# Tap products over a zeroed tile, a memset on another engine, and a new hand order in a one-core mixer kernel

## The chip, the cores and the metric

The kernel runs on one core of a Trainium2 chip. A core has five instruction queues that run side by side and meet only through semaphores: TensorE (PE, matrix products into PSUM; its weight loads are listed apart as PEld), VectorE (DVE), ScalarE (ACT), GpSimd (POOL) and SyncE (SP, which here only starts DMA transfers). Each queue works strictly in the order in which its instructions were written. The metric is the device time of one execution in microseconds; the reference point is the median over several executions.

## The reference

Two branches read the same tensor `q` (2048 tokens of 640 channels) and are mixed by a gate per token:

```python
x = A_q
g = sigmoid((x * gate_w).sum(-1, keepdims=True))
# branch a
k_shift = sum over t of k_pad[:, t:t+S, :] * shift_k[:, ks-1-t]      # ks = 4 taps
kv = k_shift * v
y = irfft(rfft(kv, 2S) * rfft(ssm_k, 2S))[:, :S] + kv * ssm_D         # a long convolution
a = q * y
# branch b
h = gelu(layernorm(x) @ w1)             # 640 -> 640, then four channel groups shifted by +1, -1, +2, -2 tokens
x1 = x + shifted(h) @ w2                # 640 -> 640
b = x1 + gelu(layernorm(x1) @ w3) @ w4  # 640 -> 1536 -> 640
out = g * a + (1 - g) * b
```

Inputs and output are bf16.

## The kernel before

`build` writes the work down as 784 tasks (one to twenty-odd instructions each), numbered as they are added. Each task has a name, an engine or a choice of engines, what it reads, writes and needs in buffers, and a duration for the planner. `ORDER` (lines 36 to 66) is one long hand-kept list of these numbers, with a letter behind a number where the task takes another than its first engine (`a` ACT, `v` DVE, `p` POOL). All tasks are emitted in that order, so `ORDER` fixes the order within every engine's queue. `Plan.place` (lines 147 to 220) goes through the list once with the planned durations and hands out the buffers: PSUM has eight banks, used singly or in pairs (pool `U`).

The same pass decides how many **fill** products are put ahead of a task on PE. A fill (lines 254 to 256) multiplies a tile of zeros, `FZ`, by itself, 128 rows by 512 columns, into a PSUM bank that nobody reads; it only keeps PE occupied while it would wait. Their number is the planned waiting time divided by a planned fill time: 0.43 us up to the planned moment `WARM` = 7.5 us, 0.22 us after it. Fills end when task `w1.0.0` has taken over the bank.

The stages, by task name:

- **Start.** `ldx` loads `q` by pairs of token tiles, `ldsk` loads the long filter `ssm_k` in five blocks, `ldw1`, `ldw2...`, `ldk`, `ldv` the rest; a number of small tasks on POOL, DVE and ACT make the identity, the all-ones tile `ONE`, and the table of cosines `TRIG` (`phase`, `phsmall`, `phand`, then `sin` on ACT).
- **Taps.** `ldCJ` loads `shift_k` as one row of 2560 values in one partition (tile `CJR`). For each tap j, `cjb.j` (line 484) multiplies the first row of `ONE` by that row on PE, which copies the tap to all 128 partitions of PSUM (512 and 128 columns, array rows 1 of 128); `cj.j` evacuates it to SBUF.
- **Layer norm 1.** `st1` (statistics, ACT or DVE), `rs1` (POOL), `nm1` (normalise, ACT or DVE), `tr1` (ten PE transposes), `ev1`/`evh` (evacuation of the transposed tile and of its shifted copy).
- **Filter.** `trh.cb` is 32 PE transposes of a block of `ssm_k`, `evt` evacuates; `s1h` and `s1hr` are the first transform step of the filter, `e1h` its evacuation.
- **Branch b.** `w1.G.part` and its gelu `g1`, then `w2`, `x1` (DVE, adds the product to `x`), `sq`, `ve2`, `st2` (POOL), `nm2`, `dt2` (DMA transposes), `w3`, gelu `g2`, `w4`, `t2`.
- **Branch a.** `kv3` to `kv0` on DVE: eight passes each over 128 x 2560 values, which form `k_shift * v`; `kz` zeroes the three leading rows of `K` in one partition, which only `kv0` reads (its taps j > 0). Then `s1x`, a round trip through DRAM (`wFx`, `rF`), `s2`, the products `pa`/`pb`, `s3`, another round trip (`wG`, `rG`), `s4`, and the last DVE steps `yq`, `ad`, `ax`, `fo` and the stores `st`.
- `bperm` permutes the cosine table (128 x 2048) for a DMA transpose `dbt` that `s4` needs; in the kernel before it runs on POOL (`701p`), and `kz` too (`4p`).

In the order before, PE's queue starts `fill cjb.0 cjb.2 cjb.3 cjb.1 trh.3 sgm trh.0 tr1.0 tr1.2 trh.4 trh.1 tr1.14 trh.2 tr1.4 w1.0.0`, and SP's queue `ldCJ ldx0 ldx4 ldx14 ldx2 ldsk3 ldsk0 ldgw ldx6 ... ldw1`. `sgm` (line 679) is a small product of the gate's weights, which `ldgw` loads.

Of the kernel before, what the change touches and what calls it, by code (L numbers as in the profile page):

```python
# [10 lines left out]
ACT = mybir.ActivationFunctionType  # L11
ALU = mybir.AluOpType
BF16 = mybir.dt.bfloat16
# [23 lines left out]
0 5 14 12 26 28 25 2 8 9 3 1 7 10 75p 68v 13 21 65p 27 6 42 86v 84v 39 69 22a 17 76v 24 18a 15 16a 58v 56v 19  # L37
66a 71v 11 400 212 29 67 38 77 78a 79 23 43 401v 81v 87 70a 57 80a 36 394 20a 40 59 395v 72 74v 41 94v 37 82 92a
61v 83v 402 85 73a 60a 88v 403a 396 397v 62 63v 93 398 89a 64a 96a 95 399v 33 97v 32 213 90 124 44 91a 47 457
128 118v 458a 119 125 116v 408 46 30 461 463 98 99v 130 129 117 404 100v 101 464a 462a 102v 35 34 407 104v 31  # L40
131 126 132 121v 405 103 445 127 465 133 453 466a 105v 146 120v 140 45 54 454a 446a 141 143 106 147 137 107v 459
144 138 110a 108a 409 410 145 111 113v 49 411 154 460a 155 152 148 149 150 109 134 153 451 449 151 468 165 112a
135 412 452a 159 450a 467 166 122 406 139 114 136 156 123a 413 115v 160 51 447 142 218 157 469 48 219 414 214
215 475 470a 222v 448a 50 473 53 168 170 476a 456 471 417 418 419 169 474a 220a 477 176 472a 172 177 162 478a
174 163 224 173 455 420 416 481 487 171 221 225 175 421 226v 488a 483 216 484a 480 187 188 181 182 482a 479 164
223 415 184 185 485 489 228a 190 422 423 424 493 4p 427 486a 490a 227 501 428 429 430 192 52 229 194 191 198
494a 497 502a 193 495 199 196 230 491 498a 492 197 195 499 200 201 496a 431 203 204 500a 432 426 505 425 158 161
506a 231 250 251 248 262 433 434 504 511 509 503 249 236 438 244 510a 512a 245 437 439 440 441 442 237 238 239
55 513 246 443 514a 247 517 436 435 444 507 508a 252 253 519 234 520a 235 523 524a 240 515 241 242 525 518a 516
521 232 206 207 526a 522a 243 178 527 263 209 528 210 233 264a 529 167 533 534v 530a 731 535 268 536a 531 532v  # L50
537 538a 265 205 208 260 540 256 269 539 258 211 179 254 266v 267 270v 272v 271 356 701p 183 261 273 186 546 541
562 217 189 312 313 202 180 306 316v 307 314v 547 308a 257 549 259 573 255 350 274 550v 542 548a 544 545v 280
310a 275 276 543a 563 281 565 574 282 277 557 309 564a 575a 292 551 578 552 594 558 560 283 566v 293 559v 561a
605 278 279 351 352v 576 579 581 582a 580v 577a 296 567 317 284 553 311 297 285 555a 568 554v 288 595 583 606
608 289 584 607a 315 609a 610 294 295 357 318 596v 589 626 611 613 614v 340 612a 637 585 360v 586v 319 713 590
642 341 615 587a 286 591a 569 592 287 330 571v 616 570a 593a 290 621 331 597 598a 638 643 338 556 599 644a 639v
353 600 320 339 321 640 645 641a 646v 291 334 622 627 572 628a 623v 629 336 601 630v 624 602v 335 354a 603a 653
674 647 332 617 625a 337 619a 658 648 358a 669 355 685 588 618a 298 631 632 299 654 655v 604 702 333 656 328
657a 659 661 322 660a 662v 670 329 620 675 676a 672 323 324 671v 690 633 325 673v 634a 635v 326 663 677 649 664
361 327 346 679 636 359 678a 686 650a 651a 665 652 687a 666a 680 688 347 667v 691 681 668 692a 689v 695 693 694a  # L60
683a 342 696 697 682a 684 699a 698v 343 300 700 304 344 302 345 305 301 303 730 712 735 703 732 736 733 362 717
# [22 lines left out]
class Plan:  # L84
# [62 lines left out]
    def place(self, order):  # L147
# [8 lines left out]
        for i in order:  # L156
# [33 lines left out]
            else:  # L190
                d = t.dur
                if e == "PE":
# [162 lines left out]
def build(env, nc, io):  # L355
# [19 lines left out]
    def dma(name, nbytes, fn, issue=0.58, **kw):  # L375
        return add(name, "SP", issue, fn, nbytes=nbytes, **kw)
# [41 lines left out]
    add("kz", {"POOL": 1.7, "DVE": 0.6}, 0, lambda t: (nc.vector if t.on == "DVE" else nc.gpsimd).memset(env["K"][0:1, 0:3, :], 0.0),  # L418
# [620 lines left out]
```

## Time and profile before

| what | us |
|---|---|
| executions of the kernel before | 231.32, 231.49, 232.72 |
| median | 231.49 |
| the profiled execution, its own time | 232.78 |
| its span, from the first instruction to the last | 231.0 |
| PE idle behind its first transposes, up to its last product | 3.5 |
| DVE idle in 0 to 20, 20 to 40, 40 to 60, 60 to 80, 80 to 100 | 4.9, 3.5, 1.9, 0.6, 0.3 |
| ACT idle in the same stretches | 7.2, 2.2, 1.8, 3.3, 1.0 |

How to read the profile: its page gives busy times, the span in 40 slices, the chain of work that ended last, and groups of instructions by source line. An answer of the trace by line L256 is the fills (recorded at the helper's line), L487 the tap products, L796 the filter's transposes, L562 the transposes of `x`, L637 and L641 `w1`, L663 `w2`, L851 and L864 the first transform step, L757 `w3`, L771 and L778 `w4`. Times in a chain and in a timeline are microseconds from the start of the span. Busy matmul times overlap, so the distance between starts, which the chain shows, is the price of a matmul in a stream. A figure in brackets at the end of a timeline row is the idle time ahead of that instruction and what ended it.

### The profile page before, as it was taken

What the parts mean: (1) busy time and instruction counts of PE and PEld (TensorE: products, weight loads), DVE (VectorE), ACT (ScalarE), POOL (GpSimd) and SP (SyncE); (2) the same over time, 40 slices, a digit from 0 to 9 for tenths busy, and PEclk for the clock granted to TensorE, in tenths of its full rate; (3) what the DMA queues carried; (4) which work ended last, traced back from release to release, by engine and by line L of the source; (5) the groups of instructions that cost most, each with busy time, mean ns of one, the idle gap of its engine ahead of it and who ended that gap; (6) DMA issues with size and microseconds to landing.
All of it is one profiled execution on the core that took longest, in us unless ns stands there. A gap on an engine that the chain in (4) does not pass through costs nothing.

```text
span 231.0 us, 5209 instructions
## 1 busy us (share of the span) xinstructions
PE 222.0 (96%) x2077; PEld 105.0 (45%) x2077; DVE 190.9 (83%) x269; ACT 154.0 (67%) x223; POOL 44.6 (19%) x92
## 2 busy tenths in 40 slices
PE   7999989999997999999999999999999999999992
PEld 1268834545443343344543333334344554445551
DVE  7949598899999999999468999898986238788993
ACT  4894799988988799979558898897965000532000
POOL 5378055513071007006421000000000000000000
PEclk9999999999999999999999999999999999999999
DMA  4999997099897899977999997999964496789623
GB/s 141 273 349 328 280 265 249 3 292 207 279 286 157 280 267 351 324 258 210 196 334 322 222 362 168 237 409 290 281 208 152 140 371 225 219 264 305 173 64 85
DMA packets 41450, 56.74 MB, mean 246 GB/s; under 512 B 15953, under 2 KB 31570, under 8 KB 41426
## 3 DMA queue, kind: packets, MB, share of 16 engines
q1 hardware_dynamic: 41426, 56.41, 84.3%
q8 instruction: 16, 0.26, 0.5%
q14 instruction: 8, 0.07, 0.1%
HBM read 34.90 MB, written 18.35 MB: 231 GB/s over the span
## 4 chain that ended last, share of the span: by engine, by line
PE 89%; DVE 5%; ACT 2%; POOL 1%; issue 1%; DVEq 0%; POOLq 0%; ACTq 0%
PE PS L757 24%; PE PS L771 17%; PE PS L663 10%; PE PS L637 7%; PE PS L898 5%; PE PS L256 5%; PE PS L796 4%; PE PS L926 4%; PE PS L851 3%; PE PS L778 3%; PE PS L641 2%; PE PS L964 2%; PE PS L562 1%; DVE QO L984 1%; PE PS L487 1%; DVE W L978 1%
## 5 line engine op out<-in xcount | busy, mean ns | idle before, releaser
L764 ACT ACTIVATE h2T<-PS 128x512 bf16<-128x512 f32 x48 | 27.8, 602 | 25.5 <-PE PS L757 22.4
L771 PE MATMUL PS<-W,h2T 128*128 128x512 bf16 (+1 forms) x288 | 40.1, 299 | 0.0
L387 ACT CAST FS<-PS 128x1024 bf16<-128x1024 f32 x38 | 37.3, 1016 | 3.3 <-issue 1.4
L757 PEld LDWEIGHTS <-W 128*128 128x128 bf16 x240 | 21.0, 98 | 31.0 <-issue 9.6
L771 PEld LDWEIGHTS <-h2T 128*128 128x128 bf16 x288 | 22.2, 98 | 18.8 <-issue 1.5
L387 ACT CAST XH<-PS 128x1024 bf16<-128x1024 f32 x24 | 23.9, 1014 | 8.2 <-PE PS L898 7.4
L757 PE MATMUL PS<-x1nT,W 128*128 128x512 bf16 x120 | 29.2, 380 | 0.0
L757 PE MATMUL PS<-XB,W 128*128 128x512 bf16 x120 | 28.3, 380 | 0.0
L913 DVE TENSOR_TENSOR PP<-XH 128x2048 bf16<-128x2048 bf16 x20 | 23.5, 1218 | 0.3
L816 DVE TENSOR_TENSOR VC<-K,VC 128x2560 bf16<-128x2560 bf16 x16 | 23.5, 1485 | 0.2
L663 PE MATMUL PS<-W,hsT 128*128 128x512 bf16 (+1 forms) x160 | 23.2, 299 | 0.0
L389 DVE CAST XH<-PS 128x1024 bf16<-128x1024 f32 x16 | 19.4, 1221 | 3.0 <-PE PS L898 2.5
L637 PE MATMUL PS<-xnT,W 128*128 128x512 bf16 x80 | 19.1, 380 | 1.1 <-ACT hsT L654 0.7
L786 DVE TENSOR_TENSOR x<-PS,x 128x640 bf16<-128x640 f32 x12 | 9.6, 821 | 11.6 <-PE PS L771 11.5
L730 POOL TENSOR_TENSOR r<-v,MH 128x2 f32<-128x2 f32 x8 | 8.2, 1021 | 54.8 <-DVE v L725 52.1
L820 DVE TENSOR_TENSOR VC<-VC 128x2560 bf16<-128x2560 bf16 x12 | 17.9, 1490 | 0.2
L663 PEld LDWEIGHTS <-hsT 128*128 128x128 bf16 x160 | 12.7, 98 | 11.5 <-issue 1.1
L970 DVE SCALAR_TENSOR_TENSOR W<-PS,GG,QO 128x640 bf16<-128x640 f32 x16 | 13.4, 877 | 2.0 <-PE PS L964 2.0
L387 ACT CAST GS<-PS 128x1024 bf16<-128x1024 f32 x13 | 13.0, 1017 | 2.9 <-PE PS L926 2.7
L256 PE MATMUL PS<-C 128*128 128x512 bf16 x32 | 13.0, 548 | 1.2 <-DVE C L477 1.2
L654 ACT ACTIVATE hsT<-PS 128x512 bf16<-128x512 f32 x20 | 11.6, 609 | 3.8 <-PE PS L637 2.4
L778 PE MATMUL PS<-W,h2T 128*128 128x128 bf16 (+1 forms) x96 | 13.6, 299 | 0.0
(110 smaller groups left out, 300.5 us busy)
## 6 DMA issues: line engine op xcount, KB each, us to landing
FH<-FS SPq DMA_DIRECT2D x8, 640.0 KB, 4.4
FXD<-FS SPq DMA_DIRECT2D x8, 640.0 KB, 5.5
FX<-FXD SPq DMA_DIRECT2D x10, 512.0 KB, 6.2
FX<-FH SPq DMA_DIRECT2D x10, 512.0 KB, 6.1
GX<-GD SPq DMA_DIRECT2D x8, 640.0 KB, 5.0
W<-in_B_w_dram SPq DMA_DIRECT2D x2, 1920.0 KB, 10.6
GD<-GS SPq DMA_DIRECT2D x8, 480.0 KB, 5.5
x<-in_A_q_dram SPq DMA_DIRECT2D x16, 160.0 KB, 4.0
```

The costliest lines, as they stand in the source:

```text
L256: nc.tensor.matmul(env.PS[:, t.fill_at, :], lhsT=Z[:, 0:128], rhs=Z[:], start=True, stop=True)
L387: nc.scalar.copy(out=out, in_=in_)
L389: (nc.vector if t.on == "DVE" else nc.gpsimd).tensor_copy(out=out, in_=in_)
L637: nc.tensor.matmul(m[:, b, :], lhsT=W[:, 0, kb, 160 * fb:160 * fb + 128], rhs=rhs(kb, shifts[fb]), start=(kb == 0), stop=(kb == 4))
L663: nc.tensor.matmul(m[:, c0:c1], lhsT=env["hsT"][:, o.buf["hs"][0], fb, 128 * (s % 4):128 * (s % 4) + 128], rhs=env["W12"][:, 1, fb, c0:c1] ...
L757: nc.tensor.matmul(env.PS[:, t.buf["U"][0], :], lhsT=env["W3"][:, kb, 128 * fb:128 * fb + 128], rhs=env.nT(int(nP[-1]))[:, :, kb, :], star ...
L764: nc.scalar.activation(out=env["h2T"][:, o.buf["h2"][0], fb, :], in_=env.PS[:, t.buf["U"][0], :], func=ACT.Gelu_apprx_tanh)
L771: nc.tensor.matmul(m[:, c0:c1], lhsT=env["h2T"][:, o.buf["h2"][0], fb, 128 * (s % 4):128 * (s % 4) + 128], rhs=env["W4"][:, fb, c0:c1], st ...
L778: nc.tensor.matmul(env.PS[:, t.buf["U"][0], 0:c1 - c0], lhsT=env["h2T"][:, o.buf["h2"][0], fb, 128 * (s % 4):128 * (s % 4) + 128], rhs=env ...
L816: nc.vector.tensor_tensor(out=VC[:, o], in0=env["K"][:, a + 3 - j:a + 7 - j, :], in1=w, op=ALU.mult)
L820: nc.vector.tensor_tensor(out=VC[:, 1], in0=VC[:, 1], in1=VC[:, 2], op=ALU.add)
L913: nc.vector.tensor_tensor(out=env["PP"][:, o.buf["PP"][0], a, :].rearrange("p (b c) -> p b c", b=2), in0=X.unsqueeze(1).broadcast_to([P, 2 ...
```

## The change

1. **Tap products.** The tile `CJR` now has 128 partitions. A new task `cjz` on ACT copies the zero tile `FZ` five times over it (128 x 2560); `ldCJ` then loads the taps into its first partition, and each `cjb.j` multiplies all of `ONE` (128 x 128 ones) by all of `CJR`, so that 127 rows of zeros are added. Its mode in the planner is that of the full products. `ldCJ` has to wait for `cjz`, which has to wait for the memset of `FZ`.
2. **Fills.** The rule that put at least two fills ahead of every `cjb` is gone, and while the planned time is below `WARM` the number of fills is taken at 0.85 of the planned wait.
3. **Memset.** `kz` may run on DVE only, and stands second in DVE's queue.
4. `bperm` may no longer run on POOL; the order puts it on DVE.
5. **Order.** All of `ORDER` is new, with other engines for some of the tasks.

```diff
-                            t.fill = int((at - max(free[e], 0.8)) / FILL_US[0])
+                            t.fill = int(0.85 * (at - max(free[e], 0.8)) / FILL_US[0])
...
-                    if self.kept is not None and t.name[:3] == "cjb":
-                        t.fill = max(t.fill, 2)
...
-    add("kz", {"POOL": 1.7, "DVE": 0.6}, 0, lambda t: (nc.vector if t.on == "DVE" else nc.gpsimd).memset(env["K"][0:1, 0:3, :], 0.0),
+    add("kz", "DVE", 0.55, lambda t: nc.vector.memset(env["K"][0:1, 0:3, :], 0.0),
...
-    dma("ldCJ", 5120, lambda t: nc.sync.dma_start(out=env.early("CJR", [1, 4 * D], BF16), in_=io["sk"].rearrange("d j -> (d j)").unsqueeze(0)),
+    add("cjz", "ACT", 2.2, lambda t: nc.scalar.copy(out=env.early("CJR", [P, 4 * D], BF16).rearrange("p (a b) -> p a b", b=512),
+                                                    in_=env.early("FZ", [P, 512], BF16).unsqueeze(1).broadcast_to([P, 5, 512])),
+        use=[zeros], w=["CJR"], roles=("C0",))
+    dma("ldCJ", 5120, lambda t: nc.sync.dma_start(out=env.early("CJR", [P, 4 * D], BF16)[0:1, :], in_=io["sk"].rearrange("d j -> (d j)").unsqueeze(0)),
         w=["CJR"], roles=("C0",))
...
-                nc.tensor.matmul(env.Uf(t.buf["U"][0])[:, c0:c1], lhsT=env["ONE"][0:1, :], rhs=row[:, j, c0:c1], start=True, stop=True)
-        tb = add(f"cjb.{j}", "PE", 0.3, cjb, r=["CJR", "c0"], use=[fill], acq=("U",), mode="r32", roles=("C0",))
+                nc.tensor.matmul(env.Uf(t.buf["U"][0])[:, c0:c1], lhsT=env["ONE"][:], rhs=row[:, j, c0:c1], start=True, stop=True)
+        tb = add(f"cjb.{j}", "PE", 0.3, cjb, r=["CJR", "c0"], use=[fill], acq=("U",), mode="f", roles=("C0",))
...
-    add("bperm", {"ACT": 2.5, "DVE": 1.4, "POOL": 3.5}, 0, lambda t: copy(
+    add("bperm", {"ACT": 2.5, "DVE": 1.4}, 0, lambda t: copy(
```

What the new order does to each queue, read from the two lists (numbers behind the new task are one higher, 785 in all):

- **PE** starts `fill sgm cjb.3 cjb.1 cjb.0 trh.4 cjb.2 tr1.2 trh.0 trh.1 tr1.0 trh.2 trh.3 tr1.14 tr1.4 s1h.4 w1.0.0`. Ahead of `w1.1.0` now stand also `w2.0`, `w2.2`, `w2.3`, `tr1.8` and `s1h.5`, and no longer `s1hr.0`. `w2.15` stands behind `s1x.0`, `s1x.3` and `s1xr.0`. The places where one kind of product (rows and columns of the array in use) follows another are 117 instead of 121.
- **SP** starts `ldx2 ldx0 ldx14 ldgw ldCJ ldsk4 ldx4 ldw2b2 ldsk0 ldsk1 ldw2b3 ldx6 ldw2b0 ldD ldsk2 ldsk3 ldw1`; `ldw1` is its 17th task as before.
- **ACT** starts `cjz warm st1.3 st1.0 cj.1 cj.3 sin cj.2 cj.0 evt.4 nm1.0 st1.7 ev1.0 evt.2 st1.6 e1h.4 ev1.14 e1h.5 g1.0.0`. Up to `g1.1.0` it has `cjz`, three `st1`, one `evt` and one `ev1` more than before, and four `nm1` and one `evh` fewer.
- **DVE** starts `zeros kz warm0 phase1 phase0 phsmall phand`. In all it has five `nm1`, four `nm2`, one `evh`, `kz` and `bperm` more, and one `st1`, two `ev1`, one `evt` and one `e3` fewer. `bperm` stands behind `e1x.1`, ahead of `ve2.6` and `nm2.5`.
- **POOL** loses `kz` and `bperm`.

More of the change, by code (lines that the diff above doesn't have):

```diff
@@ L42 @@
[L42 to L46, printed above, removed]
@@ L484, in cjb @@
         def cjb(t, j=j):
-            row = env.early("CJR", [1, 4 * D], BF16).rearrange("o (d j) -> o j d", j=4)
+            row = env.early("CJR", [P, 4 * D], BF16).rearrange("o (d j) -> o j d", j=4)
             for (c0, c1) in ((0, 512), (512, 640)):
-                nc.tensor.matmul(env.Uf(t.buf["U"][0])[:, c0:c1], lhsT=env["ONE"][0:1, :], rhs=row[:, j, c0:c1], start=True, stop=True)
-        tb = add(f"cjb.{j}", "PE", 0.3, cjb, r=["CJR", "c0"], use=[fill], acq=("U",), mode="r32", roles=("C0",))
+                nc.tensor.matmul(env.Uf(t.buf["U"][0])[:, c0:c1], lhsT=env["ONE"][:], rhs=row[:, j, c0:c1], start=True, stop=True)
+        tb = add(f"cjb.{j}", "PE", 0.3, cjb, r=["CJR", "c0"], use=[fill], acq=("U",), mode="f", roles=("C0",))
         add(f"cj.{j}", {"ACT": 0.7, "DVE": 0.82}, 0, lambda t, tb=tb, j=j: copy(t, env["VC"][:, 3, j, :], env.Uf(tb.buf["U"][0])[:, 0:D]),
```

45 lines of the change are left out of this document (25 added, 20 removed), and 8 rows, old and new, of the table ORDER.

## The prediction

> **What bounds the kernel now.** I read the page first, then the chain of waits.
>
> ```profile
> PE 222.0 (96%) x2077; PEld 105.0 (45%) x2077; DVE 190.9 (83%) x269; ACT 154.0 (67%) x223; POOL 44.6 (19%) x92
> PEclk9999999999999999999999999999999999999999
> ```
> ```profile
> 8.09 0.65 PE PS L487 x2
> 8.74 5.80 PE PS L256 x15
> 14.54 1.92 PE PS L796 x32
> ...
> 19.59 0.22 PE PS L256
> ```
> ```profile
> L256 PE MATMUL PS<-C x32: 379/619/634, 1.2 to 24.7; 128*128 128x512 bf16 x32
> ```
>
> PE is busy for 96% of the span, but not with work that counts: nothing except fills and taps runs on it before 14.54. So two things can make this kernel shorter: an earlier first transpose, or fewer holes behind it. The 15 fills ahead of 14.54 take 5.80 us, 0.39 each; one at 19.59 takes 0.22, and recorded durations of the same instruction go from 379 to 634 ns. PE thus ran at about half speed until shortly before 14.54, although the PEclk row says full speed throughout; that row does not show this brake. The planner costs fills behind 7.5 us at 0.22, so these 15 ran far longer than it planned. Was there data to work on?
>
> ```profile
> 1.12 5.03 SPq L382 DMA_DIRECT2D x<-in_A_q_dram  x8
> 6.20 1.06 SPq L510 DMA_DIRECT2D SK<-in_A_ssm_k_dram  x2
> 7.30 0.43 SPq L493 DMA_DIRECT2D GW<-in_gate_w_dram  x1
> ```
> ```profile
> SK<-in_A_ssm_k_dram SPq DMA_DIRECT2D x1, 512.0 KB, 3.9
> ```
>
> The last row is the DMA view cut to the filter block issued at 6.20: it landed 3.9 us later, at 10.1. The first transpose could have begun there and began 4.4 us later, behind queued fills. Next, how full the others are:
>
> ```profile
> 0.00:20.00 20.00, 18.73 (x118) 8.34 (x119) 15.11 (x40) 12.78 (x21) 12.04 (x42) 1.00 0.84 266
> 20.00:40.00 20.00, 19.29 (x220) 12.17 (x218) 16.50 (x35) 17.79 (x22) 9.21 (x19) 1.00 0.96 278
> 60.00:80.00 20.00, 18.75 (x148) 8.23 (x141) 19.36 (x22) 16.75 (x25) 4.67 (x4) 1.00 0.92 252
> 100.00:120.00 20.00, 18.95 (x153) 9.88 (x151) 15.06 (x32) 13.14 (x26) 6.22 (x11) 1.00 0.94 251
> ```
>
> The columns are stretch, length, then busy PE, PEld, DVE, ACT, POOL. DVE has 8.4 us free in the first 40 us and 0.6 in 60 to 80; ACT has 9.4 free in the first 40. PE's holes behind 14.54 sum to 3.5 us: 0.7 in 20 to 40, 1.25 in 60 to 80, 1.05 in 100 to 120 and 0.5 later. A gain at the start reaches the end only if DVE, nearly full from 60 us on, also starts its long passes earlier; its free time lies where it waits for PE, so it can.
>
> **The change, part by part, against the profiled 232.78.** *The start.* SP's first issue is at 0.72; eight `x` issues took 5.03, so the new order's six take 3.8; `ldgw` adds 0.43, the taps' load some 0.35, and `ldsk4` goes out near 5.4. With 3.9 to landing the first block is there at 9.3. `trh.4` also stands behind `sgm` and three taps, and three pairs of taps fill the PSUM that the fill bank leaves, so one must be evacuated first.
>
> ```profile
> x<-in_A_q_dram SPq DMA_DIRECT2D x3, 160.0 KB, 3.2
> ```
> ```profile
> GW<-in_gate_w_dram SPq DMA_DIRECT2D x1, 1.2 KB, 5.6
> ```
> ```profile
> L387 ACT COPY HT<-PS 128x2048 bf16<-128x2048 bf16 x1 | 1.9, 1866 | 0.0
> L387 ACT COPY xnT<-PS 128x1280 bf16<-128x1280 bf16 x3 | 3.7, 1225 | 3.6 <-DVE xnT L389 3.5
> L387 ACT CAST VC<-PS 128x640 bf16<-128x640 f32 x4 | 2.7, 686 | 3.6 <-PE PS L487 3.6
> L425 ACT ACT_TABLE_LOAD x1 | 1.3, 1283 | 0.7 <-PEq L1023 0.7
> L477 DVE MEMSET C<- 128x256 uint32 x1 | 0.3, 272 | 0.0
> ```
>
> The gate's weights, issued near 4.5, land between 7.7 (3.2 to landing, as the `x` loads issued early) and 10.1 (5.6, as `ldgw` itself among later traffic); the three taps take 3 x 0.65, the first evacuation overlaps all but 0.69 at most. So `trh.4` starts between 10.3 and 12.8. Two things more can hold it: half speed, which makes its 1.92 us nearly twice that, and fills, whose number the new planner pass sets and which I have not worked out. The best case is 10.3, a gain of 4.2; the worst is 14.5, none. I take 11.5 and full speed soon after it: **3.0 gained**, nearer to the landing rows than to the old start.
>
> The new wait is `ldCJ` behind `cjz`. Both longer ACT copies differ by 0.64 us over 768 columns, so 2560 columns cost 1866 + 512 x 0.83 = 2.3 us. It starts when `FZ` is cleared, near 1.15, or behind a table load at 2.0, and ends at 3.5 to 4.3; SP comes to `ldCJ` near 4.9. So it waits for nothing; were it late, `ldsk4` and all later loads in SP's queue would be late by as much. `kz` on DVE: 960 words against 256 in 272 ns make 1.0 us. It delays DVE's chain of phases by that much, with one `st1` (1.15 us) given to ACT in return; what covers it is DVE's free time in the first 20 us. Without that cover it costs 1.0 once.
>
> *The stage behind it.* Up to `g1.1.0` ACT has more to do. With 2.3 for `cjz`, 1.87 and 1.23 for `evt` and `ev1`:
>
> ```profile
> L541 ACT ACTIVATE JK<-x 128x640 bf16<-128x640 bf16 x5 | 3.7, 738 | 0.0
> L542 ACT ACTIVATE JK<-x,SA 128x640 bf16<-128x640 bf16 x5 | 4.1, 828 | 0.2
> L554 ACT ACTIVATE xn<-x,NB,RS 128x640 bf16<-128x640 bf16 x6 | 5.4, 916 | 0.0
> 39.49 0.63 ACT L654 ACTIVATE hsT<-PS 128x512 bf16<-128x512 f32 x1
> ```
>
> Three `st1` are 3 x 1.57, nearly 2 each with their read-outs, so 5.9; four `nm1` fewer save 3.7, the halo copies 1.4. The balance is 2.3 + 1.9 + 1.2 + 5.9 - 3.7 - 1.4 = 6.2, against 9.4 free. It fits, with 3.2 to spare. DVE's sum up to `kv0.v` is equal within 0.5 us (five `nm1`, one `evh` and `kz` more; two `ev1`, `evt` and `st1` fewer). `ldw1` is SP's 17th task as before: no gain or loss. I put nothing down for this stage, and its risk into a rival.
>
> *`kz` and `bperm` off POOL.*
>
> ```profile
> 68.24 1.69 POOL L418 MEMSET K<- 1x1920 bf16 x1
> 68.33 1.78 DVE L556 TENSOR_SCALAR xn<-x,r,SB 128x640 bf16<-128x640 bf16 x1 [0.40 <-POOL SB L732]
> 70.03 0.80 DVE L670 SCALAR_TENSOR_TENSOR x<-PS,x 128x640 bf16<-128x640 f32 x1
> 70.90 0.40 PE L864 MATMUL PS<-HT,TRIG 64*128 64x128 bf16 x8 [0.91 <-DVE x L670]
> ```
> ```profile
> L556 DVE TENSOR_SCALAR xn<-x,r,SB x9: 428/442/2156, 59.2 to 138.0; 128x640 bf16<-128x640 bf16 x9
> ```
> ```profile
> 41.42 1.36 PE PS L663 x10
> ...
> 105.36 13.16 PE PS L771 x96
> ```
>
> A normalisation that otherwise takes 0.44 took 1.78 while POOL cleared `K`'s rows, and ended 0.18 after POOL did. The `x` sums behind it came 1.34 late, and PE stood 0.91 us waiting for them and 0.34 more behind that, the 1.25 of this stretch. With the memset elsewhere that hole should close, unless in the new order another wait ends last there: between 0 and 1.25, I take **1.0**, since it is a direct link. The slowest of the nine, 2.16, ran beside `bperm` on POOL and lost 1.72 to it. On DVE a copy of that size from PSUM takes 1.23:
>
> ```profile
> L389 DVE COPY HT<-PS 128x2048 bf16<-128x2048 bf16 x4 | 4.9, 1225 | 5.9 <-PE PS L796 5.9
> ```
>
> So `bperm` costs DVE 1.2 and gives back 1.7, and it stands where PE has 13.16 us of `w4` ahead of it: nothing. Without that cover, 1.2.
>
> *The hole at 103 to 105.* `w2.15`, 1.36 us like every `w2`, now stands between the first `s1x` and the last two, where PE waited 1.05: between 0 and 1.05, **0.5**.
>
> ```profile
> 36.96 1.19 PE PS L637 x5
> ...
> 63.65 1.08 PE PS L637 x5
> ```
>
> *Changes of kind.* Five products behind another kind take 1.19, behind their own 1.08: 0.11 each. Four fewer: 0.4, of which **0.3** lie behind the start.
>
> *New holes.* The order is new everywhere, so waits that were covered can open. Their bounds are none and the 3.5 us of the old order; I take **1.2 lost**. The sum is 3.0 + 1.0 + 0.5 + 0.3 - 1.2 = 3.6, from 232.78 to 229.2. The profiled execution lies 1.29 above the median of 231.49. I count half of that for the clock's start, which this change also touches, and so take 0.6 off: **228.6**.
>
> **The rivals.** *The clock stays late.* If PE idles ahead of `sgm` or a tap, or the fills are still too many, the first transposes run slow or begin near 14.5. For it speaks that 15 unbroken fills took 5 us to bring full speed, and that nothing forces fills now; against it, that all-row products replace one-row ones. Then only the later terms count (1.0 + 0.5 + 0.3 - 1.2 = 0.6), with the 0.6 to the median: 232.78 - 0.6 - 0.6 = 231.6.
>
> *ACT takes over the first 40 us* (the slower side). The place is ACT's queue up to `g1.1.0`; the price is 6.2 us more work plus 1.28 if the zero copy brings a table load of its own. It decides when ACT's free time before that gelu cannot fall below 3.2: queue order counts, since `st1.7` and `st1.6` wait for the sixth load ahead of `ev1.0` and the gelus. If none of the 9.4 is used, `g1.1.0` moves from 39.5 to 47.0, while the PE work newly put ahead of it (three `w2` of 1.36, and smaller steps) excuses 4.1: 3.4 late, and the hole at 70 is then no gain: 232.78 + 3.4 - 0.6 = 235.6. With 3.4 of it used, nothing is lost or won.
>
> *Transposes do not count.*
>
> ```profile
> L562 PE MATMUL PS<-ID,xn x80: 219/219/230, 18.9 to 53.3; 128*128 128x128 bf16 x80
> ```
>
> If the transposes start slow and do not bring full speed themselves, the five `trh` (5 x 1.92 = 9.6 us fast) take twice that, 9.6 more against the 3.0 won: 232.78 + 6.6 - 0.6 - 0.6 = 238.2. Against it, the 13 us from 14.54 on are nearly all transposes, and none of the 80 of `x`, which begin at 18.9, took over 230 ns. The Trainium skill, TensorE: Matmul & The Clock Gate, Part 4, says that transposes do not count as busy for the gate and that full speed does not engage in them. By that rule this rival would come true whenever the taps end before the clock is up; the trace bears it out badly, since by the rule the speed should have fallen in those 13 us.
>
> *Everything fits:* 4.2 + 1.25 + 1.05 + 0.4 without new holes, 6.9 less: 225.3.
>
> **How the numbers follow.** Forecast 0.55, clock late 0.20, ACT 0.13, transposes 0.04, everything fits 0.08. The forecast's own spread is 226.5 to 230.5. About 1% (2.3 us) is what a measurement can tell from no change, so faster means below 229.2: two thirds of the forecast, all of the last case and a tenth of the late clock, together 0.47; slower (above 233.8) is transposes and most of ACT, 0.15; the rest, 0.38, is the same. The range of 226.0 to 232.6 leaves out the transposes, most of ACT and half of the best case, under 0.2.
>
> **What would show it.** Right: the first L796 row at 10 to 12.5; `L637` beginning near 25; no DVE row of L556 above 0.5 us; no hole at `x L670` before `w1.3`; the first gelu before 30. Wrong: fills in a long row up to 14, L796 pieces of 3 us or more, ACT's first `L654` at 32 or later, or PE holes of more than 3.5 us behind the start.

## The result and the profile after

The kernel after takes 228.88 us (median of six executions, 228.79 to 230.59), the kernel before, in the same comparison, 231.9 (231.32 to 232.86, six executions). The ratio is 0.9883, with a 95% interval of 0.9843 to 0.9922: 3.0 us faster, against a forecast of 228.6. The profiled execution of after took 228.79 with a span of 227.0, that of before 232.78 with 231.0; its traces thus differ by 4.0, a little more than the medians. Four later executions lie far off the others of their kernels and enter no ratio (545.41 of the kernel before, 427.45 of `b_cap4`, 256.63 of `b_taps`, and 424.77 of `a_first`, which was its profiled one, so that its trace isn't read); they move the medians below by some 0.1 us.

Lines of after are one higher than before's from the tap products on (L488 taps, L638 `w1`, L797 the filter's transposes), and the fills stand at L254. First the page, then PE's timeline of the start (start, duration, engine, line, operation, tiles, count, and in brackets the idle time ahead and what ended it):

```profile
PE 216.4 (95%) x2051; PEld 105.9 (47%) x2070; DVE 188.7 (83%) x275; ACT 155.4 (68%) x222; POOL 35.2 (15%) x90
```
```profile
1.17 4.92 PE L254 MATMUL PS<-C 128*128 128x512 bf16 x12 [1.17 <-DVE C L475]
8.02 0.17 PE L683 MATMUL PS<-GW,ONE 128*128 128x5 bf16 x1 [1.93 <-DMA GW<-in_gate_w_dram]
8.04 1.86 PE L488 MATMUL PS<-C,ONE 128*128 128x512 bf16 x6
...
10.69 1.99 PE L797 MATMUL PS<-ID,SK 128*64 128x128 bf16 x32
...
13.39 1.02 PE L254 MATMUL PS<-C 128*128 128x512 bf16 x4
...
27.09 1.24 PE L638 MATMUL PS<-xnT,W 128*128 128x512 bf16 x5
```

The same view of before, its first transposes and its first `w1` product:

```profile
14.47 1.99 PE L796 MATMUL PS<-ID,SK 128*64 128x128 bf16 x32
...
28.02 1.24 PE L637 MATMUL PS<-xnT,W 128*128 128x512 bf16 x5
```

The first transposes come 3.8 us earlier, but the first product with `w1` only 0.9 earlier: most of the early start is gone 16 us later. Between the two, PE before had its transposes lined up and took 13.6 us; PE after takes 16.4. By the starts in the timeline some 1.0 of these 2.8 us are work that the new order put in between (`cjb.2` 0.7 and `s1h.4` 0.3), 0.8 are waits and 0.6 more fills. Yet the end of the span moved by 4.0. The rest must come from behind the start. The view of waits, those of PE that it lists from the whole span, before:

```profile
PE PS L256 <- DVE C L477: 1.2, 1, 1.2
PE PS L864 <- DVE x L670: 0.9, 1, 0.9
PE PS L637 <- ACT hsT L654: 0.7, 1, 0.7
PE PS L851 <- DVE x L670: 0.5, 2, 0.4
PE PS L864 <- DVE FS L389: 0.5, 1, 0.5
PE PS L637 <- DVE x L670: 0.3, 1, 0.3
PE PS L926 <- ACT GS L387: 0.3, 1, 0.3
```

and after:

```profile
PE PS L683 <- DMA GW<-in_gate_w_dram: 1.9, 1, 1.9
PE PS L254 <- DVE C L475: 1.2, 1, 1.2
PE PS L563 <- ACT FS L385: 0.5, 1, 0.5
PE PS L797 <- ACT xnT L385: 0.5, 1, 0.5
PE PS L664 <- DVE x L671: 0.3, 1, 0.3
PE PS L927 <- ACT XH L385: 0.2, 1, 0.2
PE PS L899 <- ACT GS L385: 0.2, 1, 0.2
PE PS L779 <- issue: 0.2, 1, 0.2
PE PS L254 <- issue: 0.2, 1, 0.2
```

A row gives the total in us, how often, and the longest. Behind the first `w1` product the waits of before sum to 3.2 us (all but the first row); after has 1.4 there (the rows of L563, L664, L927, L899 and L779). That is 1.8 us. The two holes that the prediction named are closed, as two stretches of 20 us show (columns as in the prediction; for before 18.75 and 18.95 us of PE):

```profile
60.00:80.00 20.00, 19.89 (x160) 8.79 (x161) 19.76 (x23) 18.39 (x27) 0.00 (x0) 1.00 0.78 204
...
100.00:120.00 20.00, 19.89 (x178) 9.91 (x179) 13.92 (x31) 15.01 (x28) 5.79 (x15) 1.00 0.92 255
```

The other part is the start itself. The fills' group, before and then after:

```profile
L256 PE MATMUL PS<-C 128*128 128x512 bf16 x32 | 13.0, 548 | 1.2 <-DVE C L477 1.2
```
```profile
L254 PE MATMUL PS<-C 128*128 128x512 bf16 x23 | 8.6, 514 | 1.4 <-DVE C L475 1.2 <-issue 0.2
```

PE spent 4.4 us less on fills and waited 2.6 us more at the start (1.9 for the gate's weights, 0.5 for `xnT`, 0.2 issue): 1.8 gained. (As the first `w1` product came only 0.9 earlier, another 0.9 us of work now stands ahead of it, `s1h.4` among it.) So 1.8 from the start and 1.8 from the later holes, counted on PE. The remaining 0.4 of the 4.0 is a balance: PE's other work is 1.2 us less (busy time less fills, 209.0 and 207.8), and idle time that the view doesn't list is 0.8 more. What either is made of stays open.

What sets the start now is seen in the chain of waits (start, duration, engine, tile, line), its longer pieces from 17 to 31 us:

```profile
17.44 1.92 PE PS L797 x32
...
21.12 1.23 ACT xnT L385
22.35 1.77 ACT HT L385
...
24.92 1.24 DVE HT L387
...
29.72 1.28 ACT L655
```

From 21 us on the chain runs mostly through copies out of PSUM on ACT and DVE and then through the gelu's table load, hardly through PE. An earlier first transpose does nothing for these unless the copies come earlier too.

Further on, the chain of after runs from 57 to 98 us mostly through DVE, above all its passes of `kv3` to `kv0`, where that of before runs from 60 to 103 almost wholly through PE. The last of these passes, of `kv0`, in the timeline of before and of after:

```profile
100.80 1.49 DVE L824 TENSOR_TENSOR K<-VC 128x2560 bf16<-128x2560 bf16 x1
```
```profile
96.52 1.49 DVE L825 TENSOR_TENSOR K<-VC 128x2560 bf16<-128x2560 bf16 x1
```

It starts 4.3 us earlier, and the whole gain of the span is there by then. The same holds for all thirteen traces used here: from the start of this pass to the end of the span they take 130.2 to 130.8 us, 130.2 in before and 130.5 in after. The prediction's condition, that DVE starts its long passes earlier too, was thus met.

(A correction to a number above: the kernel before has 785 tasks and the kernel after 786.)

### The profile page after: what moved, and what is told of

Read it like the earlier page. It is cut to its first block, busy times and chain, and to the rows that moved or that the text cites. A ratio compares the mean times of both kernels' runs of the same rounds, so it can differ in the third digit from the quotient of the medians.

```text
span 227.0 us, 5167 instructions
## 1 busy us (share of the span) xinstructions
PE 216.4 (95%) x2051; PEld 105.9 (47%) x2070; DVE 188.7 (83%) x275; ACT 155.4 (68%) x222; POOL 35.2 (15%) x90
## 4 chain that ended last, share of the span: by engine, by line
PE 66%; DVE 18%; ACT 7%; issue 4%; SPq 2%; DMA 2%; DVEq 0%; ACTq 0%
PE PS L758 18%; PE PS L772 17%; DVE VC L821 6%; DVE VC L817 6%; PE PS L779 5%; PE PS L664 5%; PE PS L899 5%; PE PS L927 4%; PE PS L797 3%; PE PS L965 2%; DVE x L671 2%; ACT FS L385 2%; PE PS L638 2%; DVE K L825 2%; SPq L380 2%
## 5 line engine op out<-in xcount | busy, mean ns | idle before, releaser
L772 PE MATMUL PS<-W,h2T 128*128 128x128 bf16 (+1 forms) x280 | 39.9, 297 | 0.6
L758 PE MATMUL PS<-x1nT,W 128*128 128x512 bf16 x120 | 28.5, 380 | 0.0
L664 PE MATMUL PS<-W,hsT 128*128 128x128 bf16 (+1 forms) x153 | 23.0, 296 | 0.6 <-DVE x L671 0.3
L638 PE MATMUL PS<-xnT,W 128*128 128x512 bf16 x80 | 19.3, 380 | 0.0
L664 PEld LDWEIGHTS <-hsT 128*128 128x128 bf16 x160 | 12.8, 98 | 11.8 <-issue 1.5
L731 POOL TENSOR_TENSOR r<-v,MH 128x2 f32<-128x2 f32 x8 | 7.0, 874 | 58.9 <-DVE v L726 56.7
L385 ACT CAST GS<-PS 128x1024 bf16<-128x1024 f32 x14 | 13.6, 1017 | 2.8 <-PE PS L927 2.8
L671 DVE SCALAR_TENSOR_TENSOR x<-PS,x 128x640 bf16<-128x640 f32 x16 | 13.0, 819 | 0.7 <-PE PS L664 0.7
L779 PE MATMUL PS<-W,h2T 128*128 128x128 bf16 (+1 forms) x94 | 13.1, 297 | 0.2 <-issue 0.2
```

The lines of the kernel that those rows point to most:

```text
L385: nc.scalar.copy(out=out, in_=in_)
L638: nc.tensor.matmul(m[:, b, :], lhsT=W[:, 0, kb, 160 * fb:160 * fb + 128], rhs=rhs(kb, shifts[fb]), start=(kb == 0), stop=(kb == 4))
L664: nc.tensor.matmul(m[:, c0:c1], lhsT=env["hsT"][:, o.buf["hs"][0], fb, 128 * (s % 4):128 * (s % 4) + 128], rhs=env["W12"][:, 1, fb, c0:c1] ...
L671: nc.vector.scalar_tensor_tensor(out=x, in0=env.Uf(t.buf["U"][0])[:, 0:D], scalar=1.0, in1=x, op0=ALU.mult, op1=ALU.add, accum_out=SS("S1" ...
L758: nc.tensor.matmul(env.PS[:, t.buf["U"][0], :], lhsT=env["W3"][:, kb, 128 * fb:128 * fb + 128], rhs=env.nT(int(nP[-1]))[:, :, kb, :], star ...
L772: nc.tensor.matmul(m[:, c0:c1], lhsT=env["h2T"][:, o.buf["h2"][0], fb, 128 * (s % 4):128 * (s % 4) + 128], rhs=env["W4"][:, fb, c0:c1], st ...
```

## The experiments

Each kernel was timed beside the kernel before; every ratio is to that, with its 95% interval. Four explanations were tested. START: the early first transposes carry the gain. ORDER: the new order's later part carries it. PORT: moving the memset costs at the start what it gains at 70. DATA: PE's queue at the start waits for loads and copies whatever stands in it.

| kernel | what it is | us | ratio (interval) |
|---|---|---|---|
| `b_cap4` | before, 15 fills cut to 4 | 231.41 | 0.9962 (0.9934 to 0.9990) |
| `b_taps` | before with the wide taps | 233.31 | 1.0048 (1.0014 to 1.0082) |
| `b_kz` | before with the memset second on DVE | 232.79 | 1.0021 (1.0001 to 1.0040) |
| `b_parts` | before with all parts, old order | 231.23 | 0.9976 (0.9945 to 1.0007) |
| `a_tapsold` | after with the old taps and fills | 231.80 | 0.9980 (0.9953 to 1.0006) |
| `a_kzpool` | after, memset on POOL | 229.81 | 0.9906 (0.9877 to 0.9935) |
| `a_bppool` | after, `bperm` on POOL | 229.29 | 0.9867 (0.9847 to 0.9888) |
| `a_warm1` | after, one table load less | 229.47 | 0.9897 (0.9868 to 0.9926) |
| `a_first` | after, fills only ahead of `sgm` | 228.49 | 0.9830 (0.9802 to 0.9857) |
| `a_nofill` | after without fills | 228.66 | 0.9857 (0.9816 to 0.9899) |
| `bp_first` | `b_parts` without fills | 229.69 | 0.9887 (0.9862 to 0.9913) |
| `b_first` | before, fills only at the taps | 230.83 | 0.9938 (0.9917 to 0.9959) |

### One part at a time in the old order

**`b_cap4`**

```diff
+                    if t.name == "trh.3":
+                        t.fill = min(t.fill, 4)
```

> The kernel before, with at most 4 instead of 15 fills ahead of the first filter transpose; taps, memsets and order untouched. Theory START (the lost time is queued slow fills in front of data that has landed): the first L796 row moves from 14.5 to 10.5 to 11, and the time falls by 1 to 3 us as DVE's passes start earlier. Rival ORDER (the old order has no use for an earlier start, ACT or loads end last there): first transposes early, time within 0.5 us. Rival CLOCK (fills are needed to bring full speed): transposes and first w1 products run slower, no gain or a loss.

Measured: 0.9962, some 0.9 us. The first transposes began at 11.31, waiting for the filter's load, and the first gelu at 30.41 instead of 32.03; the span was 229.4. So an earlier first transpose is worth something in the old order too, a little less than START forecast, but of the 3.2 us won there half is left at the gelu (1.6).

**`b_taps`** (the new task `cjz` behind `warm` on ACT, `ldCJ` behind the third `x` load)

```diff
-                            t.fill = int((at - max(free[e], 0.8)) / FILL_US[0])
+                            t.fill = int(0.85 * (at - max(free[e], 0.8)) / FILL_US[0])
-                    if self.kept is not None and t.name[:3] == "cjb":
-                        t.fill = max(t.fill, 2)
...
+    add("cjz", "ACT", 2.2, ...
-                nc.tensor.matmul(..., lhsT=env["ONE"][0:1, :], rhs=row[:, j, c0:c1], ...
+                nc.tensor.matmul(..., lhsT=env["ONE"][:], rhs=row[:, j, c0:c1], ...
```

> The kernel before with the new taps alone (zeroed tile, all rows, no forced fills, 0.85), the taps' load moved behind three pairs of x loads, the zero copy behind the first table load; the rest of the order is the old one. START: first transposes at 10.5 to 12 instead of 14.5 and 1 to 3 us less. ORDER: early transposes, but less than 0.5 us gained. Rival PORT (what counts is the memset and the copy leaving GpSimd): no gain either.

Measured: 1.0048, slower by 1.1 us. The taps stood in one run from 6.99 on and the first transposes began at 12.77, 1.7 earlier than before, but the first `w1` product at 28.64, 0.6 later. The planner set 31 fills. Seven of them ran from 17.09 to 18.60, ahead of transposes whose normalised tiles were written by 16.9; that these fills make up the loss is likely but wasn't tested. START fails here.

**`b_kz`** (the memset second in DVE's queue)

```diff
 ORDER, by task name
-  iota warm0 ldCJ zeros ldx0 ...
+  iota warm0 ldCJ zeros kz/v ldx0 ...
-  kv2.v s1x.12 kz/p kv1.m3 ...
+  kv2.v s1x.12 kv1.m3 ...
```

> The kernel before with only the memset of K's rows on VectorE, second in its queue. PORT: the 1.78 us normalisation falls to 0.44, the hole of 1.25 us at 70 closes, 1.0 to 1.3 us less. If another wait ends last there: the stretch is gone and less than 0.4 us is gained. START expects nothing from this run.

Measured: 1.0021; nothing gained, against 1.0 to 1.3 forecast by PORT. The hole at 70 was closed: the wait on `x` at L864 (0.9) and the one behind it (0.3) are gone from PE's waits. It was given back at the start. The timeline of `b_kz`:

```profile
1.28 0.86 DVE L417 MEMSET K<- 1x960 uint32 x1
...
1.76 2.75 POOL L408 TENSOR_SCALAR_AFFINE_SELECT ID<-ID 128x128 bf16<-128x128 bf16 x1
...
4.46 0.20 POOL L413 MEMSET ONE<- 128x128 bf16 x1
...
4.72 0.72 PE L486 MATMUL PS<-C,ONE 1*128 1x512 bf16 x2 [1.62 <-POOL C L414]
```

and that of before:

```profile
1.76 1.18 POOL L409 TENSOR_SCALAR_AFFINE_SELECT ID<-ID 128x128 bf16<-128x128 bf16 x1
2.90 0.20 POOL L414 MEMSET ONE<- 128x128 bf16 x1
```

POOL's `affine_select` took 2.75 instead of 1.18. In before it started during DVE's first phase operation (1.57 to 2.80) and ended 0.14 behind it; in `b_kz` it started during the memset and ended 0.16 behind the second phase operation (3.14 to 4.35). That it waited for DVE is read from these rows, not tested apart. `ONE` came 1.56 late, and with it the taps and, behind 15 fills as before, the first transposes (15.37) and the first gelu (33.15, 1.1 late). The memset is off one path and its successor on DVE is on another. In the kernel after the order makes `ONE` ahead of the identity (at 2.49 and 2.69), so the taps don't wait for it.

**`b_parts`** (all three parts, as above and `bperm` on DVE)

```diff
-    add("kz", {"POOL": 1.7, "DVE": 0.6}, 0, ...
+    add("kz", "DVE", 0.55, ...
-    add("bperm", {"ACT": 2.5, "DVE": 1.4, "POOL": 3.5}, 0, ...
+    add("bperm", {"ACT": 2.5, "DVE": 1.4}, 0, ...
```

> The kernel before with the new taps, the memset on VectorE and the permutation on VectorE, in the old order (only the tokens that these need are moved). START plus PORT without the new order: 2 to 4 us less, near the changed kernel. ORDER: well short of the changed kernel, 0 to 1.5 us less.

Measured: 0.9976, not told apart from no change. The parts alone, in the old order and with the planner's own 37 fills, aren't shown to make the kernel faster. At this point ORDER looked right.

### One part taken back in the new order

**`a_tapsold`**

```diff
-                            t.fill = int(0.85 * (at - max(free[e], 0.8)) / FILL_US[0])
+                            t.fill = int((at - max(free[e], 0.8)) / FILL_US[0])
+                    if self.kept is not None and t.name[:3] == "cjb":
+                        t.fill = max(t.fill, 2)
...
-    add("cjz", "ACT", 2.2, lambda t: nc.scalar.copy(...
+    add("cjz", "ACT", 0.01, lambda t: None, ...
-                nc.tensor.matmul(..., lhsT=env["ONE"][:], ...
+                nc.tensor.matmul(..., lhsT=env["ONE"][0:1, :], ...
```

> The kernel after in its own order, with the tap products of the kernel before: one row, forced fills, the planner's factor for fills back at 1.0, and no zero copy on ACT. The sigmoid product still waits for the gate's weights until about 8.0; three pairs of taps of 0.65 us with two forced fills of 0.4 each ahead of them take 4.3 us instead of 1.9. START (the wide taps win at the first transposes, and the end gets it) expects the first transposes at about 12.5 instead of 10.7 and 228.9 + 1.5 = 230.4. ORDER (what moved behind the start carries the gain, the form of the taps hardly matters) expects a later first transpose, but ACT 3.6 us freer (no zero copy of 2.33, no second table load of 1.28), the first gelu at 31 as before, and 228.9 to 229.3. That ACT bounds the start would show as a first gelu before 30.5 and less than 228.5.

Measured: 231.80, most of the gain gone, and more lost than START had expected. Its timeline on PE:

```profile
13.99 2.04 PE L797 MATMUL PS<-ID,SK 128*64 128x128 bf16 x32
...
31.51 1.24 PE L638 MATMUL PS<-xnT,W 128*128 128x512 bf16 x5
```

The first transposes are 3.3 late against after, the first `w1` product 4.4, and the span is 4.4 longer (231.4): between these two executions a delay at the start passes to the end in full. This one lies 1.4 above its median, so the usual loss is less, 2.9 by the medians and 2.3 by the ratios. ORDER's forecast of 228.9 to 229.3 falls: with so late a start the new order isn't told apart from before. ACT had 3.6 us less to do, and that won nothing.

**`a_kzpool`**

```diff
-    add("kz", "DVE", 0.55, ...
+    add("kz", {"POOL": 1.7, "DVE": 0.6}, 0, ...
 ORDER, by task name
-  zeros kz warm0 ...
+  zeros warm0 ... st2.2 kz/p ...
```

> The kernel after with the memset of k's rows back on POOL, behind st2.2, as it stood before; nothing else changed. HOLE (prediction's term of 1.0 for it) expects the normalisation beside the memset at 1.7 to 1.8 us again, a hole of about 1.2 us on PE near 68, and 228.9 + 1.0 = 229.9 or more. PORT (the memset on DVE at 1.25 costs 0.86 us of DVE's phase chain and stretches POOL's work beside it, so that its gain is given back at the start) expects the start 0.5 to 1.0 earlier (first gelu at 30.0 to 30.5), the hole at 68 all the same, and 228.6 to 229.1 in all.

Measured: 229.81, 0.9 above after by the medians and 0.5 by the ratios, whose intervals overlap. The profile shows both sides. The first `w1` product was at 26.76, 0.3 earlier than in after; then, in the timeline of DVE and POOL:

```profile
59.57 1.69 POOL L415 MEMSET K<- 1x1920 bf16 x1
```
```profile
60.07 1.37 DVE L556 TENSOR_SCALAR xn<-x,r,SB 128x640 bf16<-128x640 bf16 x1
```

In after that normalisation takes 0.44 (at 60.29). It ended 0.18 after the memset, as the one of 1.78 did before, though in another place of the order; the `kv` pass behind it was 0.7 later than in after at 72 us and the span 0.7 longer. The Trainium skill, SBUF — State Buffer, "SBUF: two separate sides", says that a GpSimd operation and a VectorE operation in a two-port mode take a shared pair of ports exclusively, for the whole instruction, and that the other one waits; both pairs of rows agree with that, if the normalisation runs in such a mode, which no row names. HOLE holds in kind; its size is 0.5 to 0.9 (0.7 in the profile), not 1.0 or more, and of the 1.2 forecast on PE only 0.45 shows (19.44 us of work in 60 to 80, 19.89 in after). PORT's 228.6 to 229.1, with a first gelu by 30.5, isn't met: the gelu was at 30.79.

**`a_bppool`**

```diff
-    add("bperm", {"ACT": 2.5, "DVE": 1.4}, 0, ...
+    add("bperm", {"ACT": 2.5, "DVE": 1.4, "POOL": 3.5}, 0, ...
 ORDER, by task name
-  bperm/v
+  bperm/p
```

> The kernel after with the permuted copy for the w4 stage back on POOL, as before. The prediction put nothing down for it: 13 us of PE work stand ahead of it either way, and a normalisation beside it takes 2.2 instead of 0.44 us. That expects 228.5 to 229.3 and no new PE hole between 96 and 116. A rival, DVE BOUND (DVE's queue sets the pace from 56 to 98, so 1.2 us less on it shows if the copy stands within that stretch, and 1.7 lost to the port shows the other way), expects kv0.v to begin 0.5 or more later than 96.5 and 229.4 or more.

Measured: 229.29, span 227.0 as in after. The prediction's "nothing" holds. DVE BOUND, as forecast, falls: the last pass of `kv0` begins at 96.43, not 0.5 later than in after. That DVE's queue sets the pace there isn't refuted by it.

**`a_warm1`**

```diff
 ORDER, by task name
-  zeros kz warm0 fill cjz iota phase1 ldx2 phase0 warm ldx0 ...
+  zeros warm0 warm cjz kz fill iota phase1 ldx2 phase0 ldx0 ...
```

> The kernel after with the warming activation ahead of the zero copy on ACT, so that one table load stands at the start and not two: ACT has 1.28 us less to do before the first transposed copies. ACT-START (ACT's queue eats most of the start's gain, 3.8 us at the first transposes becoming 1.0 at the first gelu) expects the first gelu 0.8 to 1.3 earlier, near 30.0, and 228.0 to 228.4. DVE-CHAIN (DVE's eight pass chain from 53 on sets the later gain, whatever ACT does) expects the first gelu earlier by as much but kv0.v at 96.5 as in after, and 228.7 to 229.1. That neither moves (the first transposed copies wait for PE, not for ACT) expects the first gelu at 31.0.

Measured: 229.47, span 227.2, the first gelu at 30.89 instead of 31.02. ACT did its first statistics 1.2 us earlier and then waited longer for DVE and PE. So ACT's work as such is not what eats the start, and that reading of the chain of waits fell: ACT stands on the chain at 21 us, but there it has waited 2.2 us for `xnT` from DVE. The third forecast, that neither moves, holds. DVE-CHAIN isn't tested by this kernel, since the gelu didn't move.

### Fills left out

**`a_first`**

```diff
-                for _ in range(t.fill):
+                for _ in range(t.fill if t.name in ("sgm", "cjb.3") else 0):
```

> The kernel after with only those fills that stand ahead of the sigmoid product and the first taps (12 of 23); the 11 behind them, 3.6 us in the records between 9.7 and 27.1, are left out. DATA (what PE does between 10.7 and 27.1 waits for loads and for the copies out of PSUM, and the fills only stand in those waits) expects the first product with w1 at 27.1 less 0.5 at most, idle time in place of the fills, and 228.5 to 229.0. FILLS (they stand in PE's queue ahead of work that is ready, as the 15 did before the change) expects that product 2 to 3.6 earlier and 225.3 to 227. CLOCK (they hold the clock up) expects a granted clock below 1.00 behind 13 and the 80 transposes of x above 0.10 us each.

Measured: 228.49. By its time DATA holds: the 11 fills behind `sgm` only stood in waits. Its forecasts for the first `w1` product and the clock stay open here, without a trace; `a_nofill` shows them. It is the lowest median of all, but its interval overlaps that of after, so it isn't told apart from it.

**`a_nofill`**

```diff
-                for _ in range(t.fill):
+                for _ in range(0):
```

> The kernel after with no fill at all: PE's first work is the sigmoid product near 8.0, then taps, then transposes. It measures what the fills do to the clock. If PE's first work starts the clock as any other, it expects slow products to about 12 (granted 0.5) and full speed from then on, the first transposes at 10.7 to 11.2 in 1.9 to 2.0 us, and 228.5 to 229.5 (225.5 to 227 if the fills only cost time). By the Trainium skill, TensorE: Matmul & The Clock Gate, Part 4, transposes would not raise the clock: then it would stay at half until the first products with w1 at 27 or later, the 80 transposes of x (5.6 us in all) and the taps would take nearly twice as long, and the whole 233 or more.

Measured: 228.66, the same as after within the spread. PE's timeline, and the durations of the transposes of `x` from the view of one source line, cut to three windows (minimum, median, maximum in ns, first and last start):

```profile
13.72 1.22 PE L563 MATMUL PS<-ID,xn 128*128 128x128 bf16 x10 [0.78 <-ACT VC L385]
14.87 3.82 PE L797 MATMUL PS<-ID,SK 128*64 128x128 bf16 x64
18.62 1.09 PE L563 MATMUL PS<-ID,xn 128*128 128x128 bf16 x10
...
22.09 2.00 PE L797 MATMUL PS<-ID,SK 128*64 128x128 bf16 x32 [0.45 <-ACT xnT L385]
...
26.78 1.24 PE L638 MATMUL PS<-xnT,W 128*128 128x512 bf16 x5 [0.50 <-DMA K<-in_A_k_dram]
```
```profile
L563 PE MATMUL PS<-ID,xn x9: 311/311/311, 13.8 to 14.6; 128*128 128x128 bf16 x9
```
```profile
L563 PE MATMUL PS<-ID,xn x9: 219/314/314, 18.7 to 19.5; 128*128 128x128 bf16 x9
```
```profile
L563 PE MATMUL PS<-ID,xn x18: 219/219/230, 24.0 to 25.0; 128*128 128x128 bf16 x18
```

Without fills the first 20 transposes of `x` are slow (311 ns, ten in 1.2 us instead of 0.7), and the speed rises inside the group that ends at 19.5. From 13.7 to there PE did nothing but transposes, all but unbroken from 14.87 on. So transposes do bring full speed here, after some 4.5 us of them. `b_first` and `bp_first` agree: with nothing but transposes in between, the `x` transposes take 314 and 311 ns (medians) near 17 and 219 near 22.5. The Trainium skill, TensorE: Matmul & The Clock Gate, Part 4, says that transposes don't count as busy in the same way and that full speed doesn't engage for them; these rows speak against that, and the rival that rested on it falls. The forecast of full speed from about 12 on was wrong too: it came at about 19. The slow stretch cost PE some 20 x 0.045 = 0.9 us (starts (1.22 - 0.31) / 9 = 0.10 apart, at full speed 0.056), and yet the first `w1` product came at 26.78, earlier than in after. From its first transposes at 10.24 to there PE waited 2.3 us in all: 0.78 and 0.45 as shown, 0.58 for a copy to `HT` by DVE, and 0.50 that the view puts down to a load of `k`, which this product doesn't read. The second of DVE's copies to `xnT` ends at 26.63, which is a likelier cause.

**`bp_first`**

```diff
-                for _ in range(t.fill):
+                for _ in range(t.fill if t.name in ("sgm", "cjb.3") else 0):
```

> The kernel before in its old order with all parts of the change (wide taps, the memset and the permuted copy on DVE), and fills only ahead of the sigmoid product and the first taps, as in a_first: 21 of 37 are left out, some 8 us in the records between 9.0 and 27.4. FILL COUNT (the new order gains because fewer fills stand in PE's queue, not by the order itself) expects it within 1 us of a_first, 226 to 229.5. ORDER (the loads' order and the work placed behind the start carry it) expects the first product with w1 at 28 or later, PE idle where the fills were, the hole of 1.05 at 103 to 105 still open, and 230 to 231.

In the old order the first fills belong to `cjb.0`, so this edit left out all 37: it is the twin of `a_nofill`, not of `a_first`. Measured: 229.69, 1.1% (2.6 us) faster than before, where `b_parts` with its fills has 0.2%, and `a_nofill` 1.4%. Both forecasts miss by a little: 229.69 is 1.2 above `a_first` and just over FILL COUNT's 229.5, and under ORDER's 230, with the first `w1` product at 25.99 and not at 28. Most of the gain goes with FILL COUNT. Some 0.7 us is left for ORDER (1.2 in the spans, 228.1 and 226.9). PE has 18.91 us of work in 100 to 120 here and 19.72 in `a_nofill`, which is the old hole of 1.05 at that place. But the last pass of `kv0`, which ends ahead of the hole, begins at 97.49 here and at 96.17 there, 1.3 apart: the difference arises before the hole.

**`b_first`**

```diff
-                for _ in range(t.fill):
+                for _ in range(t.fill if t.name[:3] == "cjb" else 0):
```

> The kernel before in all but its fills: the 22 fills that the planner sets behind the taps (15 ahead of the first transposes, 7 later) are left out, the 10 at the taps stay. It has none of the change's parts, so it tells how much of the change's gain comes from PE's queue holding fewer fills alone. FILLS ALONE expects 229.5 to 230.3, the first product with w1 near 26 and the whole loss to the kernel bp_first (229.69) within 0.6. PARTS (the memset off POOL is worth the hole of 1.25 at 70, and the wide taps some tenths) expects the same early w1 product, the hole at 70 still there, and 230.6 to 231.4, as with the 15 fills capped at four (231.41).

Measured: 230.83, inside the forecast of PARTS; the intervals of this kernel and of `bp_first` don't meet. In 60 to 80 PE has 18.74 us of work here and 19.79 in `bp_first`: the hole at 70 is most of the parts' share. Its start, from PE's timeline:

```profile
11.67 2.04 PE L796 MATMUL PS<-ID,SK 128*64 128x128 bf16 x32 [2.93 <-DMA SK<-in_A_ssm_k_dram]
...
26.17 1.24 PE L637 MATMUL PS<-xnT,W 128*128 128x512 bf16 x5 [0.23 <-issue]
```

With nothing in front of it, the first transpose of before waits for its data until 11.67, and the first `w1` product comes at 26.17. In `bp_first` and `a_nofill` it is 25.99 and 26.78, though their first transposes begin at 10.74 and 10.24. In `b_cap4`, from 11.31, it is 26.40. So in none of these four does PE's queue reach that product before about 26, whatever stands at its head, and before's 28.02 left 2 us to win at the start, not 3 or 4.

## Why the prediction was right, step by step

The time (228.6 against 228.88) and the direction were right. Three kernels without the fills behind the taps give the parts of the gain. By the ratios, taken of 232.4, `b_first` (fills) is 1.4 us below before, `bp_first` (parts) 1.2 below that, `a_nofill` (order) 0.7 below that, 3.3 in all; the spans fall by 1.7, 1.2 and 1.2 (231.0, 229.3, 228.1, 226.9). The last step's intervals overlap; in the traces its 1.3 is there at the last pass of `kv0` already, and what in the order brings it stays open. The steps were taken in one order only, so each share holds for this order. Against the sum:

- **The start, 3.0 forecast, 1.4 (by `b_first`) to 1.8 (by the traces) measured.** This term was mis-sized. The first transposes came at 10.69, inside the forecast's 10.3 to 12.8, and the step that failed is the next one: that what is won at `trh.4` is won at the end. Signs for it were named, `L637` near 25 and the first gelu before 30; they came at 27.09 and 31.02. The stretch from `trh.4` to the first `w1` product, 13.6 us before, was taken to stay as it was; it took 16.4 in after and 14.5 to 16.5 in the four kernels with other fills, none of which reaches that product before about 26. Part of it is `cjb.2` and `s1h.4`, which the new order put there, and part waits for copies out of PSUM. Which of these waits comes first wasn't tested; `a_warm1` shows only that ACT's amount of work isn't it.
- **The landing row** was read from the execution that had the fills: 3.9 us from issue. In `b_first` the same load, issued at the same time, was waited for until 11.67, 5.5 after issue (5.4 in the DMA view, and 5.1 in `b_cap4`). The "4.4 us later" of the prediction was thus 2.8 there. Why the load took longer stays open.
- **Half speed "makes its 1.92 us nearly twice that"** was wrong. `trh.4` ran in after from 10.69 in 1.99, where the granted clock reads 0.50 (9 to 12 us) and the fills just ahead of it took 0.61 and 0.63 us; the first ones of `a_nofill` took 2.04. So the third rival's price of 9.6 us never existed.
- **`kz`, 1.0 forecast:** 1.2 by `b_first` to `bp_first`, with all parts at once and the ten fills at the taps out too, and 0.5 to 0.9 by `a_kzpool`. No normalisation of that line in after (L557) takes more than 0.45. What the prediction didn't see is that moving it to the head of DVE's queue can push the identity on POOL (`b_kz`, 1.1 lost); it named DVE's free time as the only cover.
- **The hole at 103 to 105, 0.5 forecast:** the hole closed, and PE's work in 100 to 120 rose by 0.94. That this shortened the kernel isn't shown: from the start of the last pass of `kv0` to the first `w4` product it takes 4.5 us in the seven traces of the old order and 4.6 to 4.7 in the six of the new one.
- **Changes of kind, 0.3 forecast:** no run isolates them.
- **New holes, 1.2 lost forecast:** 0.4 net. Without the two named holes before waited 1.0 behind the first `w1` product (`hsT` 0.7, `GS` 0.3); after waits 1.4. By PE's count all holes together gained 1.8 where 0.3 was forecast (1.0 + 0.5 - 1.2), and the start gained 1.8 where 3.0 was. The two errors nearly cancel, which is luck.
- **The 0.6 taken off for the profiled execution:** the traces differ by 4.0 and the medians by 3.0, so 1.0 was due. That it has to do with the clock's start isn't shown.
- **`bperm`, nothing forecast:** nothing (`a_bppool`).
- **The rivals.** Of "ACT takes over" the second table load of 1.28 did come, and cost nothing (`a_warm1`). Of "The clock stays late" the condition came in part, without the price: PE idled 1.9 us ahead of `sgm`, and the fills at 9.72 still ran at half speed, but the first transposes began at 10.69 and lost nothing by it. "Transposes do not count" is refuted by `a_nofill`.

The form of the taps matters through the fills and their place: one-row taps with forced fills in the new order cost 2.3 to 2.9 us (`a_tapsold`, by ratio and by median), while the wide taps alone in the old order cost 1.1 (`b_taps`), where the planner set its fills elsewhere. No run has one-row taps without the forced fills, so the two aren't told apart.

## What to carry to other kernels

A filler instruction is harmless only while the wait that it fills is real: 22 fills in the queue of before cost 1.4 us, the same kind of fills in after cost nothing, and planned waits don't say which it will be. Before pricing an earlier start, take the filler out of one kernel and see where the next shared point lands; what is won at the head of a queue counts only as far as that point moves. An operation moved off a busy shared resource must be checked at its new place for the same conflict with what now runs beside it.

## What was not expected of the hardware

- The granted clock doesn't show all of the slow start. Two stretches of after (the third figure from the end is the granted clock):

```profile
1.00:6.00 5.00, 4.83 (x12) 1.74 (x13) 4.76 (x17) 4.96 (x5) 3.37 (x13) 1.00 0.66 189
9.00:12.00 3.00, 3.00 (x30) 1.79 (x29) 2.35 (x10) 2.96 (x5) 2.39 (x8) 0.50 1.05 276
```

  In the first the clock reads 1.00 while the first ten of the 12 fills stand 0.42 us apart ((4.99 - 1.17) / 9); the four at 13.39 are 0.21 apart ((1.02 - 0.38) / 3). The spacing of one fixed product tells more.
- The filter's transposes (weights of 128 by 64) start 0.055 us apart at either speed ((1.99 - 0.27) / 31 in after, slow and fast alike); those of `x` (128 by 128) 0.10 and 0.056. What paces the first kind wasn't tested.
- Executions of one kernel lie up to 3 us apart with the granted clock of the whole span: of `b_parts` those with 1.00 took 230.3 to 230.7, those with 0.992 or 0.993 took 232.9 to 233.5. A profiled execution can so lie 2.2 us off the median, as it did there. It isn't a rule: of `a_first` those with 0.977 took 228.28 and 228.49, and of `a_nofill` one with 0.998 took 230.69, where those with 1.00 took 227.9 to 228.7.
